# Linear attention and a maxout FFN on one core: the softmax sums of batches 4 to 7 through DMA transposes and VectorE

## The chip, the core and the metric

The kernel runs on one core of a Trainium2 chip. Each engine (TensorE or PE for matrix products, VectorE or DVE, ScalarE or ACT, GpSimd or POOL, SyncE or SP, which here only issues DMAs) follows its own instruction list in order, and waits on semaphores for the others. The metric is the device time of one execution in microseconds, lower is better. Times that are compared with each other are medians over several executions.

## What is computed

An attention whose keys and values are first projected along the sequence from 1024 to 64 rows (matrices E and F), for 8 batches of 8 heads with head width 64. Its output, with the heads side by side, is the input of 8192 rows by 512 of a feed-forward block, where the largest of three products is taken element by element.

```python
k_proj = einsum('ks,bhsd->bhkd', E, k)
v_proj = einsum('ks,bhsd->bhkd', F, v)
scores = q @ k_proj.T / sqrt(64)
attn = exp(scores - max) / sum(exp(scores - max))      # over the 64 projected keys
x = (attn @ v_proj) with heads side by side             # 8192 x 512
h = max(max(x @ w1, x @ w2), x @ w3)                    # 512 -> 768
out = h @ w_out                                         # 768 -> 512
```

The kernel takes the exponential without subtracting the maximum, and divides after the product with v_proj: it multiplies by the inverse of the sum over the 64 keys.

## The kernel before, in words

One loop runs over the 8 batches b, and in each turn over two chunks of 512 rows. A chunk has 10 steps: six `up` steps (each makes one 128-wide slice of h: three groups of four 128x128x512 matmuls, one for each of w1, w2 and w3), then four `down` steps (six matmuls each, the product with w_out for 128 rows). In a step of `up`, ACT copies the first product from PSUM (h1s, L754), VectorE takes the larger of it and the second (m, L758), then of that and the third (hT, L699). `down` reads hT, ACT copies its result to o_sb, and after every second `down` SP issues a store of two results (L813).

The attention of the next batch, n = b + 1, is woven between these steps. The function `plan(b)` holds the order: a key (chunk, step) gives the list of functions that are called behind that step. [...] Eight PSUM banks are dealt out by a small planner, which keeps a model clock for TensorE, ACT and VectorE (`runs`, `pe`) and gives the bank that it expects to be free first. The numbers in `runs(...)` and `when` steer only this choice.

For loop turns b = 3 to 6, which prepare batches 4 to 7, the order is:

- behind (0, 1): the scores of head pairs 1 to 3 of batch n (`sc`); ACT makes the exponentials, tile pT (L230): for each pair of heads, 128 partitions (64 keys for each of two halves of the rows) by 1024. Pair 0 was made at the end of the turn before.
- behind (0, 3): `zc(n)`. Eight small matmuls (L264) with the 0/1 matrix `pick` add pT over the keys, for all head pairs, into one bank. ACT takes the logarithm (L270) and the exponential of its negative (L273), which gives the inverse. SP writes the result to a scratch buffer zd in DRAM (L276, 32 KB) and reads it back four times (L283, 512 KB each), spread over 64 partitions by a broadcast: tile zi_all.
- behind (0, 4): `qd(n + 1)`, for batches up to 7: VectorE copies q of the batch after next into q_p (L102), and SP issues a DMA transpose of 1 MB from q_p to qT (L422).
- behind (1, 2): `kvproj(n + 1)` (the projections of k and v; SP then transposes k by DMA to kpT, L538), and `vx` for pairs 0 and 1: the product of pT and v_proj (L239), and on VectorE its multiplication by zi_all into xT (L316).
- behind (1, 3): `ld(n + 2)`: GpSimd issues the loads of q, k and v for a later batch (L201), which convert from fp32 to bf16 on their way. The load of q waits for the DMA transposes qT and kpT of the batch before it (`last_T`, `turned`).
- behind (1, 6): `vx` for pairs 2 and 3, then the scores of pair 0 of batch n + 1.

SP's list in such a turn is therefore: zd, four zi_all, qT, the two stores of the first chunk, kpT, the two stores of the second chunk. In b = 6 there are no qT, kpT and loads. q_t has two buffers, k_t and v_t have one each, pT has six, zi_all one.

Of the kernel before, what the change touches and what calls it, by code (L numbers as in the profile page):

```python
# [8 lines left out]
FP32 = mybir.dt.float32  # L9
BF16 = mybir.dt.bfloat16  # L10
AF = mybir.ActivationFunctionType
ALU = mybir.AluOpType
# [3 lines left out]
def kernel(  # L16
# [13 lines left out]
    nc = tc.nc  # L30
# [7 lines left out]
    P = 128  # L38
    HALF = 64
# [3 lines left out]
    NPAIR = H // 2  # L43
    CHUNK = 512
    NCHUNK = S // CHUNK
    SPC = SI // NCHUNK
# [5 lines left out]
    att = ctx.enter_context(tc.tile_pool(name="att", bufs=2))  # L52
    scratch = ctx.enter_context(
        tc.tile_pool(name="scratch", bufs=2, space=bass.MemoryType.DRAM)
    )
# [26 lines left out]
    def bank():  # L82
        n = min(range(8), key=lambda n: free[n])
        deal((n,))
        return psum_t[:, n, :], (n,)

    def pe(dt, wait=0.0):
        clock["pe"] = max(clock["pe"], wait) + dt
        return clock["pe"]

    def runs(eng, ready, dt, ns=()):
        if eng in clock:
            clock[eng] = max(clock[eng], ready + 0.06) + dt
            for n in ns:
                free[n] = clock[eng]
            return clock[eng]
        return ready + dt
# [33 lines left out]
    qkv, qTs, kpTs, vps, pTs, zis, xTs = {}, {}, {}, {}, {}, {}, {}  # L131
# [119 lines left out]
    def zi_all(b):  # L251
        if b not in zi_alls:
            zi_alls[b] = att.tile([P, NPAIR, 2, CHUNK], FP32, name="zi_all", bufs=1)
        return zi_alls[b]

    def zc(b, queue=nc.sync):

        def f():  # L260
            t, ns = bank()
            for hp in range(2):
                for g in range(NPAIR):
                    nc.tensor.matmul(  # L264
                        out=t[32 * g:32 * (g + 1), :], lhsT=pick[:, hp, :],
                        rhs=pTs[b, g, 0][:, hp, :], start=(hp == 0), stop=(hp == 1),
                    )
            ready = pe(2 * MM + 0.1)
            zlc = att.tile([P, CHUNK], FP32, name="zlc", bufs=1)
            nc.scalar.activation(out=zlc, in_=t, func=AF.Ln)  # L270
            runs("s", ready, 0.6, ns)
            zic = att.tile([P, CHUNK], FP32, name="zic", bufs=1)
            nc.scalar.activation(out=zic, in_=zlc, func=AF.Exp, scale=-1.0)  # L273
            when = runs("s", ready, 0.63) + 9.0
            zd = scratch.tile([NPAIR, 2, 2, CHUNK], FP32, name="zd")
            nc.sync.dma_start(  # L276
                out=zd.rearrange("g h c f -> (g h c) f"),
                in_=zic.rearrange("(a r) f -> a r f", r=8)[:, 0, :],
            )
            for u in range(2):  # L280
                gs = slice(2 * u, 2 * u + 2)
                for hp in range(2):
                    queue.dma_start(  # L283
                        out=zi_all(b)[hp * HALF:(hp + 1) * HALF, gs],
                        in_=zd[gs, hp].partition_broadcast(HALF),
                    )
            for g in range(NPAIR):
                zis[b, g, 0] = zi_all(b)[:, g], when
        return f
# [39 lines left out]
    def sc(b, g, lo=0, nsi=SI, now=False):  # L329
        def f():  # L330
            t = scores(b, g, lo, nsi)
            if now:
                exps(b, g, lo, nsi, t)
            else:
                later.append(lambda: exps(b, g, lo, nsi, t))
        return f
# [72 lines left out]
    def qd(b, gs=range(NPAIR), eng="v"):  # L409

        def f():
            lo, n = gs[0], len(gs)
            if lo == 0:
                q_ps[b] = att.tile([P, NPAIR, SI, 2, D], BF16, name="q_p", bufs=1)
                qTs[b] = att.tile([P, NPAIR * SI, P], BF16, name="qT")
            q_p = q_ps[b]
            for g in gs:
                copy(
                    eng, q_p[:, g].rearrange("p si h d -> p h si d"),
                    qkv[b][0][:, 2 * g:2 * g + 2], (), 0.43,  # L420
                )
            last_T[b] = nc.sync.dma_start_transpose(  # L422
                out=qTs[b][:, lo * SI:(lo + n) * SI, :],
                in_=q_p[:, lo:lo + n].rearrange("p g si h d -> p (g si h d)"),
            )
        return f
# [67 lines left out]
    def kproj(b):  # L494
        def f():
            t, ns = bank()
            proj(b, 1, t, (LO, HI), 4 * D)
            kps[b] = att.tile([P, 2, 2 * D], BF16, name="kp")
            copy("v", kps[b].rearrange("a g x -> a (g x)"), t[:, 0:4 * D], ns, 0.43)
        return f  # L500

    def kt(b):
        def f():
            t, ns = two()
            t = t.bitcast(BF16)[:, 0]
            for gg in range(2):
                nc.tensor.transpose(
                    out=t[:, gg * P:(gg + 1) * P], in_=kps[b][:, gg, :], identity=ident
                )
            pe(0.2)  # L510

            kpTs[b] = att.tile([P, NPAIR, KP], BF16, name="kpT")
            copy(
                "v", kpTs[b].rearrange("a (y x) k -> a x y k", x=2),
                t[:, 0:2 * P].rearrange("a (x y k) -> a x y k", x=2, y=2), ns, 0.3,
            )
        return f
# [32 lines left out]
    def vproj(b):  # L550
        def f():
            t, ns = bank()
            proj(b, 2, t, (LO, HI), 4 * D)

            vps[b] = att.tile([P, H, D], BF16, name="vp")
            for hh, hs in enumerate((LO, HI)):
                i = t[hh * HALF:(hh + 1) * HALF, 0:4 * D].rearrange("a (h d) -> a h d", d=D)
                for to in range(2):
                    copy("sv"[hh], vps[b][to * HALF:(to + 1) * HALF, hs, :], i, ns, 0.4)
        return f  # L560
# [266 lines left out]
    def ld(b, which=(0, 1, 2)):  # L827
        return lambda: load(b, which)

    def plan(b):  # L830
        n = b + 1
        if b == 0:
            return {
                (0, 6): [
                    duo[1].sums, duo[1].values, duo[0].scale, duo[1].invert,
                ],
                (0, 7): [
                    qd(1, range(2)), duo[1].scale, qd(1, range(2, 4), "s"), store_now,
                ],
                (1, 1): [kproj(1)],  # L840
                (1, 2): [kt(1)],
                (1, 3): [sc(1, 0, now=True), sc(1, 1), vproj(1), ld(2)],
                (1, 4): [za(1, 0), sc(1, 2, now=True)],
                (1, 5): [za(1, 1)],
                (1, 6): [sc(1, 3, now=True)],
                (1, 7): [za(1, 2)],
                (1, 8): [za(1, 3)],
            }
        if b == 1:
            return {  # L850
                (0, 0): [qd(2)],
                (0, 3): [kproj(2), vproj(2), ld(3, (0,))],
                (0, 4): [kt(2)],
                (0, 5): [sc(2, 0, now=True), sc(2, 1, now=True), sc(2, 2)],
                (0, 6): [sc(2, 3, now=True)],
                (0, 8): [zc(2, nc.gpsimd), ld(3, (1, 2))],
                (1, 1): [qd(3)],
                (1, 3): [vx(2, 0), vx(2, 1)],
                (1, 6): [vx(2, 2), vx(2, 3)],
            }  # L860
        if b == 2:
            return {
                (0, 2): [kproj(3), vproj(3), ld(4)],
                (0, 3): [kt(3)],
                (0, 4): [sc(3, 0, now=True), sc(3, 1)],
                (0, 5): [sc(3, 2, now=True), sc(3, 3, now=True)],
                (0, 7): [zc(3)],
                (0, 8): [qd(4)],
                (1, 3): [kproj(4), vproj(4), ld(5), vx(3, 0), vx(3, 1)],
                (1, 4): [kt(4)],  # L870
                (1, 8): [vx(3, 2), vx(3, 3), sc(4, 0)],
            }
        if n == B:
            return {}
        out = {
            (0, 1): [sc(n, 1, now=True), sc(n, 2, now=True), sc(n, 3)],
            (0, 3): [zc(n)],
            (1, 2): [vx(n, 0), vx(n, 1)],
            (1, 6): [vx(n, 2), vx(n, 3)],
        }  # L880
        if n + 1 < B:
            out[0, 4] = [qd(n + 1)]
            out[1, 2] = [kvproj(n + 1)] + out[1, 2]
            out[1, 6] += [sc(n + 1, 0)]
        if n + 2 < B:
            out[1, 3] = [ld(n + 2)]
        return out

    duo = [Duo(u, SPC) for u in range(2)]

    for b in range(B):
        p = plan(b)

        def behind(ch, step):
# [61 lines left out]
```

## Time and profile before

| quantity | value |
|---|---|
| median of 3 runs | 399.08 us (398.91 to 399.47) |
| the profiled execution, its own time | 399.08 us |
| its span, first to last instruction | 397.3 us |
| granted TensorE clock | 1.00 |
| eight matmuls of `zc` in b = 3 (L264) | 180.01 to 180.55 us |
| ACT: logarithm and exponential of `zc` (L270, L273), mean of one | 597 and 630 ns |
| VectorE: multiplication by zi_all (L316), mean of one | 1220 ns |
| zd written, time to landing | 1.8 to 5.5 us, median 2.5 |
| zi_all read back, time to landing | 4.9 to 10.3 us, median 7.9 |
| qT, DMA transpose of 1 MB, time to landing | 7.2 to 22.1 us, median 12.9 (two of the eight are halves) |
| DMA engines, mean busy share in the 40 slices | mostly 9 tenths until 300 us, mostly 0 to 3 from 320 us |

A loop turn takes 46.4 us here: b = 3 begins at 168.5 us, b = 4 at 214.9, b = 5 at 261.2 and b = 6 at 307.6. In lines of the timeline the columns are the start in us, the duration in us, the engine (SPq is SP issuing DMAs), the line, the operation, what is written and read, and in brackets how long the engine was idle before and what ended that. In lines of the DMA view the columns are the queue, its packets, MB, and the time of its packets as a share of 16 engines; shares over 100% occur because packets overlap on an engine.

### The profile page before, as it was taken

What the parts mean: (1) busy time and instruction counts of PE and PEld (TensorE: products, weight loads), DVE (VectorE), ACT (ScalarE), POOL (GpSimd) and SP (SyncE); (2) the same over time, 40 slices, a digit from 0 to 9 for tenths busy, and PEclk for the clock granted to TensorE, in tenths of its full rate; (3) what the DMA queues carried; (4) which work ended last, traced back from release to release, by engine and by line L of the source; (5) the groups of instructions that cost most, each with busy time, mean ns of one, the idle gap of its engine ahead of it and who ended that gap; (6) DMA issues with size and microseconds to landing.
All of it is one profiled execution on the core that took longest, in us unless ns stands there. A gap on an engine that the chain in (4) does not pass through costs nothing.

```text
span 397.3 us, 5598 instructions
## 1 busy us (share of the span) xinstructions
PE 386.9 (97%) x2196; PEld 173.5 (44%) x2238; DVE 202.4 (51%) x309; ACT 151.9 (38%) x236; POOL 34.3 (9%) x49
## 2 busy tenths in 40 slices
PE   7899999999999999999999999999999999999996
PEld 3544443453445445444444444444444444444443
DVE  3348756751764525645374544845266443745251
ACT  2434638527222552263323532245323533132322
POOL 7350001000401100200011000200000000000000
PEclk9999999999999999999999999999999999999999
DMA  8999999987999998999979969597971138020202
GB/s 146 206 206 207 205 237 151 245 160 161 231 183 263 165 211 205 220 180 210 214 202 160 245 151 270 100 240 124 217 210 43 64 89 234 2 106 0 107 0 106
DMA packets 67338, 66.29 MB, mean 167 GB/s; under 512 B 31504, under 2 KB 59792, under 8 KB 67312
## 3 DMA queue, kind: packets, MB, share of 16 engines
q0 software_dynamic: 29104, 30.41, 47.4%
q1 hardware_dynamic: 38064, 35.46, 34.7%
q8 instruction: 17, 0.28, 0.3%
q10 hardware_dynamic: 144, 0.07, 0.1%
q14 instruction: 9, 0.07, 0.1%
HBM read 69.73 MB, written 16.97 MB: 218 GB/s over the span
## 4 chain that ended last, share of the span: by engine, by line
PE 90%; DMA 3%; DVE 2%; POOL 2%; issue 1%; ACT 1%; DVEq 0%; ACTq 0%; POOLq 0%
PE banks L689 61%; PE banks L797 20%; DMA v_t<-in_v_dram 3%; PE banks L239 2%; PE banks L353 2%; PE banks L219 2%; PE banks L528 1%; PE banks L264 1%; DVE xT L316 1%; DVE m L758 1%; ACT zi_all L305 1%; ACT zl L299 1%; DVE hT L699 0%; POOL k_t L152 0%; POOL q_t L157 0%
## 5 line engine op out<-in xcount | busy, mean ns | idle before, releaser
L689 PE MATMUL banks<-xT,w_sb 128*128 128x512 bf16 x1125 | 255.2, 379 | 1.9 <-DVE xT L316 0.3
L689 PEld LDWEIGHTS <-w_sb 128*128 128x128 bf16 x1152 | 110.2, 98 | 136.7 <-issue 8.4
L758 DVE TENSOR_TENSOR m<-banks,h1s 128x512 f32<-128x512 f32 x90 | 62.1, 690 | 131.4 <-ACT h1s L754 88.8
L754 ACT COPY h1s<-banks 128x512 f32<-128x512 f32 x90 | 52.6, 585 | 119.6 <-PE banks L689 119.6
L797 PE MATMUL banks<-wout_sb,hT 128*128 128x512 bf16 x364 | 85.5, 380 | 1.0 <-issue 0.3
L699 DVE TENSOR_TENSOR hT<-banks,m 128x512 bf16<-128x512 f32 x90 | 62.3, 692 | 9.7 <-DVE m L758 0.5
L797 PEld LDWEIGHTS <-hT 128*128 128x128 bf16 x378 | 35.3, 98 | 48.4 <-issue 6.1
L102 ACT COPY o_sb<-banks 128x512 f32<-128x512 f32 (+2 forms) x57 | 32.9, 577 | 58.4 <-PE banks L797 50.6
L316 DVE TENSOR_TENSOR xT<-banks,zi_all 128x1024 bf16<-128x1024 f32 x28 | 33.2, 1220 | 12.8 <-PE banks L239 8.2
L230 ACT ACTIVATE pT<-banks 128x1024 bf16<-128x1024 f32 (+1 forms) x32 | 30.2, 975 | 16.2 <-PE banks L219 16.2
L201 POOL DMA_DIRECT2D q_t<-in_q_dram x7 | 6.1, 878 | 197.3 <-DMA qT<-q_p 84.9
L102 ACT CAST vp<-banks 64x256 bf16<-64x256 f32 (+1 forms) x11 | 4.7, 424 | 20.5 <-DVE kp L102 11.2
L102 DVE CAST vp<-banks 64x256 bf16<-64x256 f32 (+2 forms) x15 | 6.7, 445 | 10.0 <-ACT vp L102 7.3
L239 PE MATMUL banks<-pT,vp 64*64 64x512 bf16 (+1 forms) x128 | 10.3, 375 | 0.5 <-DVE vp L102 0.2
L102 DVE COPY q_p<-q_t 128x1024 bf16<-128x1024 bf16 x26 | 9.8, 437 | 0.0
L219 PE MATMUL banks<-qT,kpT 64*64 64x512 bf16 (+1 forms) x128 | 9.7, 372 | 0.0
L102 DVE CAST kp<-banks 128x256 bf16<-128x256 f32 (+2 forms) x9 | 4.6, 509 | 8.8 <-PE banks L528 3.5
L102 DVE COPY o_sb<-banks 128x512 f32<-128x512 f32 (+1 forms) x9 | 5.6, 640 | 5.4 <-PE banks L777 4.5
L299 ACT ACTIVATE zl<-banks 128x512 f32<-128x512 f32 (+1 forms) x8 | 6.5, 810 | 2.9 <-PE banks L239 2.7
L353 PEld LDWEIGHTS <-efT 128*64 128x64 bf16 x128 | 6.6, 110 | 2.1 <-issue 2.1
L567 PE MATMUL banks<-warm_f 128*128 128x512 f32 x8 | 5.9, 877 | 1.5 <-DVE warm_f L175 1.5
L201 POOL DMA_DIRECT2D v_t<-in_v_dram x7 | 6.3, 900 | 1.0 <-PE banks L689 1.0
(76 smaller groups left out, 136.3 us busy)
## 6 DMA issues: line engine op xcount, KB each, us to landing
out_dram<-o_sb SPq DMA_DIRECT2D x30, 512.0 KB, 3.9
zi_all<-zd SPq DMA_DIRECT2D x20, 512.0 KB, 7.9
q_t<-in_q_dram POOLq DMA_DIRECT2D x7, 1024.0 KB, 9.8
k_t<-in_k_dram POOLq DMA_DIRECT2D x7, 1024.0 KB, 17.1
v_t<-in_v_dram POOLq DMA_DIRECT2D x7, 1024.0 KB, 21.9
zi_all<-zd POOLq DMA_DIRECT2D x4, 512.0 KB, 7.6
w_sb<-in_moe_w_dram POOLq DMA_DIRECT2D x4, 384.0 KB, 11.0
k_t<-in_k_dram POOLq DMA_DIRECT2D x2, 512.0 KB, 9.1
```

The source lines that it names most:

```text
L102: done = {"v": nc.vector.tensor_copy, "s": nc.scalar.copy, "g": nc.gpsimd.tensor_copy}[eng](out=o, in_=i)
L201: dma = nc.gpsimd.dma_start(out=tiles[i], in_=view((q, k, v)[i], b))
L219: nc.tensor.matmul(out=t[c * HALF:(c + 1) * HALF, hp, 0:n * P], lhsT=k_pair(b, g)[rows], rhs=qTs[b][rows, at:at + n, :], start=True, stop= ...
L230: nc.scalar.activation(out=pTs[b, g, lo], in_=t, func=AF.Exp, scale=scale)
L239: nc.tensor.matmul(out=t[hp * HALF:(hp + 1) * HALF, c, 0:nsi * HALF], lhsT=w(rows, hp), rhs=p[rows, hp, :], start=True, stop=True,)
L316: nc.vector.tensor_tensor(out=xTs[b][:, g, lo:lo + nsi, :].rearrange("a (c s) p -> a c (s p)", c=2), in0=t, in1=zi, op=ALU.mult,)
L353: nc.tensor.matmul(out=t[hh * HALF:(hh + 1) * HALF, 0:width], lhsT=efT[:, si, (kv - 1) * KP:kv * KP], rhs=qkv[b][kv][:, heads[hh], si, :], ...
L689: nc.tensor.matmul(out=h, lhsT=w_sb[i][:, ct, jt * P:(jt + 1) * P], rhs=xTs[b][:, ct, ch * SPC:(ch + 1) * SPC, :], start=(ct == first), st ...
L699: nc.vector.tensor_tensor(out=o, in0=h, in1=other, op=ALU.max)
L754: nc.scalar.copy(out=h1s, in_=h[0][0])
L758: nc.vector.tensor_tensor(out=m12, in0=h[1][0], in1=h1s, op=ALU.max)
L797: nc.tensor.matmul(out=o_ps, lhsT=hTs[b, ch][:, jt, tt * P:(tt + 1) * P], rhs=wout_sb[:, jt, :], start=(jt == 0), stop=(jt == NJT - 1),)
```

## The change

For batches 4 to 7, `zc(n)` is no longer called (batches 2 and 3 keep it). Three new functions do its work:

- `turn_p`: SP issues a DMA transpose of each pT tile (128x1024 bf16, 256 KB) into p_T, eight blocks of 128x128 in which the rows of the sequence lie on the partitions and the keys along the free dimension. p_T uses the buffers of the tile zi0.
- `sum_p`: VectorE adds over the 64 keys, 1024 elements in and 16 out per partition (tile s_T).
- `spread_z`: VectorE inverts the 64 sums per partition (zr), transposes the 128x64 tile in 32x32 blocks (zt), SP writes zt to zd with two DMAs in pieces of 32 numbers, and reads it back with the same four zi_all DMAs as before.

Their places in the plan: pair 0 is turned behind (0, 0), pairs 1 to 3 behind (0, 2), the sums are made behind (0, 5), (0, 6) and (0, 7), and the spreading follows behind (0, 7). `qd(n + 1)` stays behind (0, 4). SP's list in such a turn becomes: four turns of pT, qT, the first store, two zd writes, four zi_all, the second store, kpT, the stores of the second chunk.

```diff
+    def turn_p(b, g):
+        def f():
+            if b not in s_T:
+                s_T[b] = att.tile([P, NPAIR, 2, SPC, 2], FP32, name="s_T")
+            p_T[b, g] = att.tile([P, 2, CHUNK // 2], FP32, name="zi0", bufs=4).rearrange(
+                "p a f -> p (a f)"
+            ).bitcast(BF16).rearrange("p (n x) -> p n x", x=P)
+            nc.sync.dma_start_transpose(
+                out=p_T[b, g], in_=pTs[b, g, 0].rearrange("p h f -> p (h f)")
+            )
+        return f
+
+    def sum_p(b, g):
+        def f():
+            nc.vector.tensor_reduce(
+                out=s_T[b][:, g].rearrange("p h s c -> p (h s) c"),
+                in_=p_T[b, g].rearrange("p n (c k) -> p n c k", c=2),
+                axis=mybir.AxisListType.X, op=ALU.add,
+            )
+            runs("v", 0.0, 1.15)
+        return f
+
+    def spread_z(b, queue=nc.sync):
+        def f():
+            n = NPAIR * 4 * SPC
+            zr = att.tile([P, n], FP32, name="zr")
+            nc.vector.reciprocal(
+                out=zr.rearrange("p (a c s) -> p a c s", c=2, s=SPC),
+                in_=s_T[b].rearrange("p g h s c -> p (g h) c s"),
+            )
+            zt = att.tile([P, n], FP32, name="zt")
+            nc.vector.transpose(out=zt, in_=zr)
+            when = runs("v", 0.0, 0.35) + 11.0
+            zd = scratch.tile([NPAIR, 2, 2, CHUNK], FP32, name="zd")
+            rows = zd.rearrange("g h c (s a r) -> (g h c s) a r", a=4, r=32)
+            for j in range(2):
+                nc.sync.dma_start(
+                    out=rows[32 * j:32 * (j + 1)].rearrange("i a r -> a i r"),
+                    in_=zt[:, 32 * j:32 * (j + 1)],
+                )
...
         out = {
             (0, 1): [sc(n, 1, now=True), sc(n, 2, now=True), sc(n, 3)],
-            (0, 3): [zc(n)],
+            (0, 0): [turn_p(n, 0)],
+            (0, 2): [turn_p(n, 1), turn_p(n, 2), turn_p(n, 3)],
+            (0, 5): [sum_p(n, 0), sum_p(n, 1)],
+            (0, 6): [sum_p(n, 2)],
+            (0, 7): [sum_p(n, 3), spread_z(n)],
             (1, 2): [vx(n, 0), vx(n, 1)],
             (1, 6): [vx(n, 2), vx(n, 3)],
         }
```

More of the change, by code (lines that the diff above doesn't have):

```diff
@@ L279, in f @@
             )
+            for u in range(2):
+                gs = slice(2 * u, 2 * u + 2)
+                for hp in range(2):
+                    queue.dma_start(
+                        out=zi_all(b)[hp * HALF:(hp + 1) * HALF, gs],
+                        in_=zd[gs, hp].partition_broadcast(HALF),
+                    )
+            for g in range(NPAIR):
+                zis[b, g, 0] = zi_all(b)[:, g], when
+        return f
+    s_T, p_T = {}, {}
+    def turn_p(b, g):
[17 more added lines that the diff above has]
+            runs("v", 0.0, 1.15)
+        return f
+    def spread_z(b, queue=nc.sync):
[15 more added lines that the diff above has]
+                    in_=zt[:, 32 * j:32 * (j + 1)],
+                )
             for u in range(2):
```

## The prediction, made before the changed kernel ran

> **What bounds the kernel now.** I read the busy shares first, then the chain of waits, then the timeline of loop turn b=4 (batch 5 is prepared there, span 215 to 261 us), and last the DMA view in stretches of 2 us.
>
> ```profile
> PE 386.9 (97%) x2196; PEld 173.5 (44%) x2238; DVE 202.4 (51%) x309; ACT 151.9 (38%) x236; POOL 34.3 (9%) x49
> PE 90%; DMA 3%; DVE 2%; POOL 2%; issue 1%; ACT 1%; DVEq 0%; ACTq 0%; POOLq 0%
> ```
>
> TensorE is never free for long: it is busy 97% of the span and holds 90% of the chain that ended last. So a TensorE instruction that goes is worth its whole time, and any wait that reaches TensorE costs its whole time too. The next view, VectorE's timeline late in b=4, tells how near such a wait is:
>
> ```profile
> 249.25 2.36 DVE L316 TENSOR_TENSOR xT<-banks,zi_all 128x1024 bf16<-128x1024 f32 x2
> 251.52 0.68 DVE L758 TENSOR_TENSOR m<-banks,h1s 128x512 f32<-128x512 f32 x1
> 252.31 0.69 DVE L699 TENSOR_TENSOR hT<-banks,m 128x512 bf16<-128x512 f32 x1
> 252.92 0.68 DVE L758 TENSOR_TENSOR m<-banks,h1s 128x512 f32<-128x512 f32 x1
> 253.70 0.69 DVE L699 TENSOR_TENSOR hT<-banks,m 128x512 bf16<-128x512 f32 x1
> 254.80 0.69 DVE L758 TENSOR_TENSOR m<-banks,h1s 128x512 f32<-128x512 f32 x1 [0.40 <-PE banks L689]
> 255.59 0.69 DVE L699 TENSOR_TENSOR hT<-banks,m 128x512 bf16<-128x512 f32 x1
> ```
>
> From the first multiplication by zi_all to the last hT tile VectorE is idle for only 0.40 us, and the down product that follows already waited 0.20 us for that hT. So if zi_all comes late, TensorE loses the delay less 0.4 us.
>
> Now the queue that brings zi_all. SP's timeline in the same turn, and the same transpose in three surroundings:
>
> ```profile
> 228.35 0.54 SPq L276 DMA_DIRECT2D zd<-zic  x1
> 231.50 2.55 SPq L283 DMA_DIRECT2D zi_all<-zd  x4
> 234.16 10.73 SPq L422 DMA_TRANSPOSE qT<-q_p  x1
> 244.99 1.00 SPq L813 DMA_DIRECT2D out_dram<-o_sb  x2
> ...
> 78.46 5.76 SPq L422 DMA_TRANSPOSE qT<-q_p  x1
> ...
> 105.31 19.73 SPq L422 DMA_TRANSPOSE qT<-q_p  x1
> ```
>
> A DMA transpose holds SP while it is issued: 5.76 us with free engines (it lands after 7.5), 10.73 us behind zi_all, 19.73 us beside loads (lands after 22.1). The DMA view says why; here are 118 to 120 us, inside the 19.73, and 82 to 84 us, inside the 5.76:
>
> ```profile
> q0 software_dynamic: 307, 0.31, 91.3%
> q1 hardware_dynamic: 308, 0.08, 29.7%
> ...
> q1 hardware_dynamic: 2195, 0.56, 124.9%
> ```
>
> q0 carries the loads in packets of 1 KB, q1 (SP's) the transpose in packets of 256 bytes. Alone, q1 moves 2195 packets in 2 us; beside loads 308, one for one with q0.
>
> **What the Trainium skill says.** "DMA: Bandwidth & Descriptors", section "Queues, rings and completion order": each DMA engine goes round its queue rows packet by packet, and takes one row's descriptors in ring order. The trace agrees: 307 against 308 above, and in b=4 qT, issued at 234.16, shows its small packets only from about 242 us, when zi_all is through. The same page, section "Anatomy of one DMA — SWDGE (gpsimd) path": DMA engines don't wait on semaphores, the issuing sequencer does; so everything behind a waiting DMA on SP waits too (in the trace zi_all is issued at 231.50, on zd's landing 3.1 us after its issue). "VectorE: DVE Perf Modes", section "The perf-mode tier table": tensor_reduce runs at one element a cycle whatever the type. No reduction is in this trace, but the multiplication over 128x1024 is 1.22 us at that pace.
>
> **The change, part by part** (batches 4 to 7, prepared in b=3 to 6).
>
> *Removed.* Eight matmuls of L264: 180.08 to 180.62 us in the chain, 0.54 us with the gap; four times 2.2 us, all on TensorE. Two ACT passes (0.60 + 0.63 us) and the old 32 KB zd write go; ACT was idle beside them, nothing for the time.
>
> *Added on VectorE.* Four sums at 1.22 us are 4.9 us a batch, behind the last hT of the first chunk (233.2 us in b=4). VectorE has no work from there to 240.3 us, so 7.1 us cover them if the turned tiles are in. Reciprocal and transpose of 128x64: the 128x64 memset is 0.11 us, a 128x128 fp32 copy 0.29; between 0.2 and 0.8 for both, I take 0.4.
>
> *Added on SP, in its order:* four turns of 1024 packets each, then qT (4096), the store of the first two down results, two zd writes (0.54 us each by the old one), four zi_all (2.55 us). Before, zd and zi_all were ahead of qT. The turns of 256 KB each issue in 1.4 us when free (a quarter of 5.76), and 6.8 us beside loads (1024 at 150 a us). The loads of a batch, some 3,100 packets, occupy q0 from about 210 to 230 us in b=4 and from 168 to 190 in b=3, just where the turns come. zd in 128-byte pieces: old landings are 1.8 to 5.5 us; I take 2.8 from the second issue. zi_all: in b=4 its four landings were 5.0 to 10.0 us after their issues, so the first half (two DMAs) is in about 7.3 us after the first issue, the second after 11.9.
>
> Sum for batch 4 (b=3): the stores before it leave the ring at about 177 us. From there q0 has 2,193 packets left (sum of the stretches to 190). At 150 a us each, loads and turns share until 191.6; 1,900 turn packets remain and take 2.7 us at 711 a us (4096 in 5.76 us): 194.3. SP leaves the turns at about 193, qT takes it to 198.8, store and zd to 200.2; zd lies behind qT and the store in the ring and lands at 203.0. First half of zi_all: 210.3. It is wanted at 202.86 less the 0.54 saved, 202.3. Stall 8.0, on TensorE 7.6. The sums end near 197.7, 4 us after VectorE had its next work, which the eight banks just cover.
>
> Batch 5: the next q load waits for kpT, which lies behind zi_all in the ring; it starts 9.1 us later, 2.0 more than TensorE's own delay. So q0 has 1,453 + 360 packets left at 222 us, shares until 234.1, turns end at 237.3, qT is issued 236.0 to 241.8, zd lands 246.0, zi_all 253.3 against 248.7: stall 4.6, cost 4.2.
>
> Batch 6, by the same steps (load 3.9 us later than its turn, 1,868 packets left at 268): turns end 283.6, qT 282.3 to 288.1, zd 292.3, zi_all 299.6 against 295.1: stall 4.5, cost 4.1.
>
> Batch 7 has neither loads nor a qT. The sums start at 325.3 and end with the inversion at 330.5; zd lands 333.3, zi_all 340.6 against 338.1. In b=6 VectorE has 1.8 us of waits to catch up: cost 0.7.
>
> Total: 7.6 + 4.2 + 4.1 + 0.7 - 2.2 = +14.4 us. The profiled span is 397.3 and that run took 399.08, which is also the median; so 413.5 us.
>
> **Rivals.** *The turns are hidden (faster).* If a turn gets through beside loads at its free pace (1.4 us), the four of batch 4 are in by 184, qT is issued 185.4 to 191.2, the sums end at 191.5, zi_all is there at 202.7 against 202.3; only the 2.2 us remain, some given back: 397.5 us. For it: a turn is a quarter of a qT, and its sums have a gap of their own. Against it: the 308 packets. It decides as soon as zi_all lands within 0.4 us of its need. *Only batch 4 loses.* If the turns of batches 5 and 6 are in by 232 and 278 us, qT starts when its copies are ready (231.8) and zi_all lands at 248.9, in time; batch 4 still gives 5 to 8: 402 to 405 us. *VectorE and the small zd pieces bind as well (slower still).* Every 1 us that the last turn or zd lands later is passed on in three batches. The page on DMA, section "Why a DMA increments its semaphore by 16 and not by 1", spreads a DMA over as many engines (16 at most) as divide both slowest dimensions; zd's destination has 4 outermost, so an estimate is four engines instead of sixteen. With 3 us each: 423 us. Against it: it is only 128 pieces in each.
>
> **How the numbers follow.** Forecast (zi_all late in three batches) 0.58, 405 to 421 us; the heavier case 0.18; only batch 4 0.12; hidden, faster, 0.12. The range 401 to 424 leaves out the faster case and the tail of the heavier one. 0.2% of 399 (0.8 us) is about what a measurement of this kernel can tell from no change: faster 0.12, same 0.02, slower 0.86.
>
> **What would show it.** Right: turns issued 4 to 7 us long in b=3, and the last one landing near 195 us; SP's qT ahead of zd and near 5.8 us long; VectorE's multiplication waiting on the DMA zi_all<-zd for some 8, 4.6 and 4.5 us; the wait of the down product's weights on hT grown by as much; b=6 nearly whole. Wrong: turns of 1.5 us beside loads, or no wait of xT on zi_all. If VectorE waits mainly on the turned tiles instead, or kpT's late landing holds the next scores, the place is wrong though the sign is right.

## The result

| kernel | median, us | lowest to highest | against the kernel before |
|---|---|---|---|
| before | 399.25 | 398.91 to 399.47 | |
| changed | 412.4 | 411.15 to 412.97 | 1.033 [1.030, 1.035] |

The change makes the kernel 13.2 us slower. The profiled execution is the fastest of the four: 411.15 us, span 409.2, where the kernel before has 399.08 and 397.3. First the page's busy shares and shares of the chain of waits:

```profile
PE 390.8 (96%) x2206; PEld 174.1 (43%) x2206; DVE 223.0 (54%) x333; ACT 147.6 (36%) x228; POOL 34.3 (8%) x49
PE 75%; DMA 14%; DVE 5%; issue 2%; POOL 1%; ACT 1%; SPq 0%; DVEq 0%; ACTq 0%; POOLq 0%
```

TensorE's share of the chain falls from 90% to 75%, and DMA's rises from 3% to 14%. Note that TensorE's busy time rose by 3.9 us although it has 32 matmuls less to do (the count of PE doesn't show that, since the trace misses some records; the weight loads, 2238 before and 2206 here, do). Part of that rise is only apparent, because 42 matmul records are missing before and none here; the rest comes back below. The places are found by cutting the span at the first `up` matmul of each loop turn:

| loop turn (prepares) | before, us | changed, us | difference |
|---|---|---|---|
| b = 3 (batch 4) | 46.38 | 54.36 | +7.98 |
| b = 4 (batch 5) | 46.39 | 47.79 | +1.40 |
| b = 5 (batch 6) | 46.39 | 49.21 | +2.82 |
| b = 6 (batch 7) | 44.29 | 43.71 | -0.58 |

Together +11.6 of the span's +11.9 us. The loss is in the three turns that carry loads; the one without them gains. In b = 3, SP's timeline (the turns have the tile name zi because p_T uses its buffers):

```profile
170.99 22.41 SPq L303 DMA_TRANSPOSE zi<-pT  x4
193.50 4.88 SPq L481 DMA_TRANSPOSE qT<-q_p  x1
198.48 0.53 SPq L872 DMA_DIRECT2D out_dram<-o_sb  x1
199.10 1.36 SPq L335 DMA_DIRECT2D zd<-zt  x2
201.88 3.45 SPq L342 DMA_DIRECT2D zi_all<-zd  x4
205.42 0.54 SPq L872 DMA_DIRECT2D out_dram<-o_sb  x1
206.06 1.21 SPq L597 DMA_TRANSPOSE kpT<-kp  x1
```

The four turns hold SP for 22.4 us, qT for 4.9 more, and only then can the sums' inverse go out. In the kernel before, the four zi_all of this turn are issued at 186.59 us. This is what VectorE and TensorE make of it, in their timelines:

```profile
192.92 1.22 DVE L310 TENSOR_REDUCE s_T<-zi 128x16 f32<-128x1024 bf16 x1 [5.08 <-DMA zi<-pT]
195.17 2.35 DVE L310 TENSOR_REDUCE s_T<-zi 128x16 f32<-128x1024 bf16 x2 [1.03 <-DMA zi<-pT]
197.55 0.55 DVE L325 RECIPROCAL zr<-s_T 128x64 f32<-128x64 f32 x1
198.14 0.24 DVE L330 STREAM_TRANSPOSE zt<-zr 128x64 f32<-128x64 f32 x1
...
210.41 2.36 DVE L375 TENSOR_TENSOR xT<-banks,zi_all 128x1024 bf16<-128x1024 f32 x2 [5.94 <-DMA zi_all<-zd]
...
216.96 0.69 DVE L817 TENSOR_TENSOR m<-banks,h1s 128x512 f32<-128x512 f32 x1 [1.41 <-PE banks L748]
```

In the same place of the kernel before, TensorE's 35 recorded matmuls follow each other without a wait:

```profile
201.22 7.94 PE L689 MATMUL banks<-xT,w_sb 128*128 128x512 bf16 x35
```

In the changed kernel:

```profile
204.74 1.67 PE L748 MATMUL banks<-xT,w_sb 128*128 128x512 bf16 x7
211.69 6.03 PE L748 MATMUL banks<-xT,w_sb 128*128 128x512 bf16 x16 [5.28 <-DVE xT L375]
```

VectorE's multiplication by zi_all waits until 210.41 us, and every m and hT behind it in VectorE's list comes after it; the banks stay full, and TensorE stands for 5.28 us. Then its next 16 matmuls take 6.03 us. In b = 4 and b = 5 the same 16 take 3.61. VectorE's inverse is ready at 198.38 us, only 0.7 us before zd goes out: the turned tiles themselves landed late, and qT and the store on SP added the rest. The view of windows, with PE, PEld, DVE, ACT and POOL busy time, then the granted TensorE clock, DMA share and GB/s, shows why:

```profile
206.40:211.69 5.29, 0.01 (x2) 0.00 (x1) 1.28 (x2) 0.00 (x0) 0.00 (x0) 0.82 1.03 226
211.69:215.00 3.31, 3.31 (x8) 1.13 (x8) 3.10 (x5) 0.00 (x0) 0.00 (x0) 0.50 0.78 233
```

After the wait the clock is 0.50: the longest wait costs 6.03 - 3.61 = 2.4 us on top of itself. That is another part of the higher busy time. So b = 3 loses 5.28 + 2.42 - 0.54 (the removed matmuls) = 7.2 of the measured 8.0 us directly; two waits of 0.2 us on other VectorE results come in the same turn. In b = 4 and 5, where TensorE's waits for xT are 1.09 and 2.53 us, a `down` product later in the turn waits 0.62 us more for its hT.

Last the view of the DMA engines, 184 to 186 us (turns beside loads) and 330 to 332 us (turns in b = 6, no loads), with the turns of these two loop turns as issues (shortest, median and longest time that one holds SP, in ns):

```profile
q0 software_dynamic: 310, 0.32, 93.0%
q1 hardware_dynamic: 313, 0.07, 29.4%
...
q1 hardware_dynamic: 1576, 0.40, 101.3%
...
L303 SPq DMA_TRANSPOSE zi<-pT x4: 1531/5349/6479, 171.0 to 189.2; - x4
...
L303 SPq DMA_TRANSPOSE zi<-pT x4: 1232/1278/1522, 321.8 to 330.1; - x4
```

### The profile page after: what moved, and what is told of

Its sections match the earlier page's. It is cut to its first block, busy times and chain, and to the rows that moved or that the text cites. A ratio compares the mean times of both kernels' runs of the same rounds, so it can differ in the third digit from the quotient of the medians.

```text
span 409.2 us, 5634 instructions
## 1 busy us (share of the span) xinstructions
PE 390.8 (96%) x2206; PEld 174.1 (43%) x2206; DVE 223.0 (54%) x333; ACT 147.6 (36%) x228; POOL 34.3 (8%) x49
## 4 chain that ended last, share of the span: by engine, by line
PE 75%; DMA 14%; DVE 5%; issue 2%; POOL 1%; ACT 1%; SPq 0%; DVEq 0%; ACTq 0%; POOLq 0%
PE banks L748 50%; PE banks L856 18%; DMA zi_all<-zd 5%; DMA v_t<-in_v_dram 3%; DMA zi<-pT 3%; DMA zd<-zt 2%; PE banks L412 2%; PE banks L219 2%; DVE m L817 2%; DVE xT L375 2%; PE banks L239 2%; DVE hT L758 1%; DVE s_T L310 1%; ACT zi_all L364 1%; ACT zl L358 1%
## 5 line engine op out<-in xcount | busy, mean ns | idle before, releaser
L748 PE MATMUL banks<-xT,w_sb 128*128 128x512 bf16 x1152 | 259.4, 382 | 9.5 <-DVE xT L375 9.2
L856 PE MATMUL banks<-wout_sb,hT 128*128 128x512 bf16 x378 | 87.3, 380 | 1.4 <-DVE hT L758 1.2
L375 DVE TENSOR_TENSOR xT<-banks,zi_all 128x1024 bf16<-128x1024 f32 x28 | 33.2, 1220 | 27.3 <-DMA zi_all<-zd 14.9
L310 DVE TENSOR_REDUCE s_T<-zi 128x16 f32<-128x1024 bf16 x16 | 18.7, 1212 | 11.0 <-DMA zi<-pT 11.0
```

Of the source, the lines that this page charges most:

```text
L310: nc.vector.tensor_reduce(out=s_T[b][:, g].rearrange("p h s c -> p (h s) c"), in_=p_T[b, g].rearrange("p n (c k) -> p n c k", c=2), axis=m ...
L375: nc.vector.tensor_tensor(out=xTs[b][:, g, lo:lo + nsi, :].rearrange("a (c s) p -> a c (s p)", c=2), in0=t, in1=zi, op=ALU.mult,)
L748: nc.tensor.matmul(out=h, lhsT=w_sb[i][:, ct, jt * P:(jt + 1) * P], rhs=xTs[b][:, ct, ch * SPC:(ch + 1) * SPC, :], start=(ct == first), st ...
L856: nc.tensor.matmul(out=o_ps, lhsT=hTs[b, ch][:, jt, tt * P:(tt + 1) * P], rhs=wout_sb[:, jt, :], start=(jt == 0), stop=(jt == NJT - 1),)
```

## The experiments

Three theories were stated before the runs. A: zi_all is late because the turns crawl beside the loads and everything behind them on SP waits, and TensorE pays that lateness. B: the added VectorE work costs. C: the turns' own traffic costs, wherever they are.

### The parts alone

**e2_sums_alone**: `zc` stays, VectorE makes sums, inverse and transpose from pT directly, and nothing uses them. No turns.

```diff
-                in_=p_T[b, g].rearrange("p n (c k) -> p n c k", c=2),
+                in_=pTs[b, g, 0].rearrange("p h f -> p (h f)").rearrange(
+                    "p (n c k) -> p n c k", c=2, k=HALF
+                ),
...
-            (0, 0): [turn_p(n, 0)],
-            (0, 2): [turn_p(n, 1), turn_p(n, 2), turn_p(n, 3)],
+            (0, 3): [zc(n)],
```

> The kernel before, zc and zi_all untouched, plus the added VectorE work alone for batches 4 to 7: four reductions, the reciprocal and the 32x32 transpose, at their places in the changed kernel, reading pT as it is (so the sums are not those over keys) and used by nothing. Theory A: 5.6 us of work in a gap of 7.1 us, no change, 399 to 400 us. Theory B: 4 to 12 us more than before.

Measured 399.59 us, ratio 1.0008 [1.0002, 1.0015]: 0.3 to 0.4 us for all four batches. B falls.

**e3_turns_alone**: `zc` stays, and the 16 turns are made where nothing waits for them.

```diff
+            (0, 3): [zc(n)],
+        out[1, 3] = out[1, 3] + [turn_p(n, g) for g in range(NPAIR)]
```

> The kernel before, zc and zi_all untouched, plus the sixteen DMA transposes of pT alone, used by nothing and issued behind kpT, at (1, 3), so that zd, zi_all, qT and kpT keep their places. Theory A: the transfers cost nothing by themselves, 399 to 401 us. Theory C (the added 4 MB of traffic slows the loads and all else): 405 us or more.

Measured 399.0 us, ratio 0.9997 [0.9989, 1.0006]. At this place the traffic costs nothing, so C falls as it was stated ("wherever they are"). The run does not test the turns in their own place, since most of them are issued here before the next loads get going. SP's timeline in b = 3:

```profile
204.09 5.53 SPq L303 DMA_TRANSPOSE zi<-pT  x4
```

That is 5.5 us for four turns instead of 22.4. Whether the turns, beside the loads, delay the loads so that somebody waits can be read from the changed kernel: from 165 us on its view of waits has none of TensorE, VectorE or ACT on a load.

### Without the loads

**e5_before_no_loads** and **e5_after_no_loads**: the same edit in both kernels. It leaves out the loads of batches 5 to 7, which are then computed from the tiles of batch 4, so the output is not the wanted one; the time alone is of use.

```diff
     def load(b, which):
+        if b >= 5:
+            if b not in qkv:
+                qkv[b] = qkv[b - 1]
+            return
```

> The kernel before with the loads of q, k and v for batches 5 to 7 left out (those batches compute with the tiles of batch 4). It is the base line of the next run. Nothing waits for these loads in the kernel before: 399 us, at most 1 us less.

> The changed kernel with the same loads left out (batches 5 to 7 compute with the tiles of batch 4), so no load runs beside the turns of batches 4 to 7. Theory A: a turn is issued in 1.3 to 1.5 us instead of 3 to 6.5, the turns are in before qT's copies are ready, qT is issued at once, the sums run without a wait in their gap, and zi_all lands within 1 us of its need in all batches: 397 to 399 us, 1 to 2 us faster than the base line without loads. If the order on SP alone were the cause (qT ahead of zd), VectorE would still wait 3 us or more for zi_all in batches 4 to 6: 405 us or more. Theory B: 412 us.

Measured 399.47 us for the first (1.0012 [1.0005, 1.0018] of the kernel before) and 397.15 us for the second (0.9953 [0.9938, 0.9968]). So without the loads the change *gains* 2.3 us, and the prediction's removed matmuls were 2.2. SP's timeline of b = 3 and the turns as issues, then VectorE's sums and its multiplication by zi_all:

```profile
170.35 10.15 SPq L307 DMA_TRANSPOSE zi<-pT  x4
184.74 4.68 SPq L485 DMA_TRANSPOSE qT<-q_p  x1
...
191.47 1.28 SPq L339 DMA_DIRECT2D zd<-zt  x2
193.54 2.60 SPq L346 DMA_DIRECT2D zi_all<-zd  x4
...
L307 SPq DMA_TRANSPOSE zi<-pT x4: 1232/1285/2399, 170.3 to 179.2; - x4
```

```profile
185.98 4.59 DVE L314 TENSOR_REDUCE s_T<-zi 128x16 f32<-128x1024 bf16 x4
202.12 2.36 DVE L379 TENSOR_TENSOR xT<-banks,zi_all 128x1024 bf16<-128x1024 f32 x2
```

Neither line of VectorE has a wait. The slow turns need the loads beside them; that is shown. (Without the loads zi_all and qT have the DMA engines to themselves too, so the 15 us by which this run is faster than the changed kernel are not due to the turns alone.) It is no way to use the change, since the loads have to be made.

### Can the order be mended?

**e1_qT_behind**: qT is issued on SP behind zi_all instead of in front.

```diff
-            out[0, 4] = [qd(n + 1)]
+            out[0, 4] = [qd_pack(n + 1)]
+            out[0, 7] += [qd_turn(n + 1)]
```

`qd_pack` is the part of `qd` that makes the copies to q_p, `qd_turn` the DMA transpose.

> The changed kernel with one order altered: the DMA transpose qT is issued behind the four zi_all instead of ahead of zd; its copies to q_p stay where they were. Theory A (zi_all is late because of what stands before it on SP, and TensorE pays the lateness): zd is issued when the VectorE work on the sums ends, 0.7 us earlier for batch 4, 1.4 for batch 5, 0.9 for batch 6, and lands some 0.8 us sooner because qT's data is no longer ahead of it in the ring; together 5 us less, of which up to 2 may be given back where qT and kpT now land close to the next scores: 407.5 to 410 us. Theory B (the VectorE work itself is what costs): unchanged, 412 us. If qT were the main cost, the wait of xT on zi_all would vanish in all three batches: 401 us.

Measured 421.37 us, ratio 1.0555 [1.0533, 1.0577]: a clear miss, 9 us slower than the change. SP's and VectorE's timelines, then the view of waits:

```profile
197.53 1.27 SPq L335 DMA_DIRECT2D zd<-zt  x2
199.60 2.60 SPq L342 DMA_DIRECT2D zi_all<-zd  x4
202.29 11.25 SPq L500 DMA_TRANSPOSE qT<-q_p  x1
213.63 0.53 SPq L890 DMA_DIRECT2D out_dram<-o_sb  x1
214.22 1.43 SPq L615 DMA_TRANSPOSE kpT<-kp  x1
...
207.07 2.36 DVE L375 TENSOR_TENSOR xT<-banks,zi_all 128x1024 bf16<-128x1024 f32 x2 [3.47 <-DMA zi_all<-zd]
...
PEld L219 <- DMA kpT<-kp: 11.7, 3, 4.6
```

zi_all came earlier, as meant (5.94 us of wait became 3.47). Here zd goes out as soon as VectorE has the inverse (197.50 us), so by an estimate from these two waits qT in front was worth some 2.5 us, and the 3.47 left come from the turned tiles and the transfers behind the sums. But behind 2 MB of zi_all qT holds SP for 11.25 us, kpT goes out at 214.22 instead of 206.06, and the scores of the next batch wait for kpT in three turns. The expectation had looked at one transfer of the queue and not at the one after.

**e6_vx_late**: zi_all is wanted later; `vx` of pairs 0 and 1 goes three steps back.

```diff
-            (1, 2): [vx(n, 0), vx(n, 1)],
+            (1, 5): [vx(n, 0), vx(n, 1)],
```

> The changed kernel with the first two multiplications by zi_all moved from (1, 2) to (1, 5), some 8 us later; nothing else. Theory A: the waits of xT on zi_all (5.9, 2.7, 4.2, 2.1 us) vanish, but kpT, which stays behind zi_all in SP's ring, now comes too late for the next scores at (1, 6), as in the run with qT behind: TensorE waits there for kpT 4 us in batch 4 and 1 to 3 us in batches 5 and 6. 404 to 408 us. If only the wait on zi_all mattered: 398 us. Theory B: 412 us.

Measured 414.01 us, ratio 1.0376 [1.0346, 1.0405]: a miss again. The second path was expected this time, but too cheap. The view of waits, then TensorE's timeline in b = 3 and in b = 5:

```profile
DVE xT L375 <- DMA zi_all<-zd: 4.4, 3, 2.2
...
PEld L219 <- DMA kpT<-kp: 11.4, 3, 4.9
...
215.86 0.64 PE L219 MATMUL banks<-qT,kpT 64*64 64x512 bf16 x4 [4.36 <-DMA kpT<-kp]
217.26 5.90 PE L856 MATMUL banks<-wout_sb,hT 128*128 128x512 bf16 x16 [0.22 <-issue]
...
316.91 0.41 PE L219 MATMUL banks<-qT,kpT 64*64 64x512 bf16 x4 [4.62 <-DMA kpT<-kp]
...
317.93 5.07 PE L856 MATMUL banks<-wout_sb,hT 128*128 128x512 bf16 x16 [0.22 <-issue]
```

The wait on zi_all fell from 14.9 to 4.4 us in all, and 11.4 us of wait on kpT stand in its place. After the waits in b = 3 and b = 5, 16 `down` matmuls take 5.90 and 5.07 us, where 18 take 4.06 in the changed kernel; the expectation had nothing for that. kpT lies behind all four zi_all in SP's ring. In the changed kernel this was covered by the wait for zi_all.

**e7_vx_late_kpT_early**: e6, and kpT goes between the two halves of zi_all: `spread_z` issues the first half, and the second (kept in `halves`) is issued behind `kvproj`.

```diff
-            out[1, 2] = [kvproj(n + 1)] + out[1, 2]
+            out[1, 2] = [kvproj(n + 1), lambda: halves.pop()()] + out[1, 2]
```

> As the run with the late multiplications, and the second half of zi_all (head pairs 2 and 3) is issued behind kpT instead of ahead of it. Theory A: kpT lands some 5 us earlier, about when the next scores want it, and both lateness paths are covered: 397.5 to 400 us, as fast as the kernel before or up to 2 us faster. If the lateness sits elsewhere (the sums on VectorE, the turns' traffic), it stays above 405 us.

Measured 404.46 us, ratio 1.0137 [1.0119, 1.0154], 4 to 7 us above the expected. Almost 10 us of e6 are recovered, and the waits of the scores on kpT are down from 11.4 to 0.8 us, which shows the second path. It isn't all: in b = 3 the second half of zi_all is now late.

```profile
216.28 2.36 DVE L381 TENSOR_TENSOR xT<-banks,zi_all 128x1024 bf16<-128x1024 f32 x2 [4.68 <-DMA zi_all<-zd]
```

**e9_second_half_later**: e7, with `vx` of pairs 2 and 3 behind (1, 8).

```diff
-            (1, 6): [vx(n, 2), vx(n, 3)],
+            (1, 8): [vx(n, 2), vx(n, 3)],
```

> All four batches on the new path in that order, and the multiplications by the second half of zi_all moved from (1, 6) to (1, 8). Theory A: batch 4's wait of 4.7 us of VectorE for it shrinks to at most 1 us: 398.5 to 401 us. If batch 4 cannot be covered (its kpT, sums or loads come too late as well): 403 us or more.

Measured 401.62 us, ratio 1.0064 [1.0046, 1.0083], just above the expected range; b = 3 is 47.55 us long against 51.35 in e7. TensorE still waits there 1.02 us for kpT and 0.92 for xT. Of the 13.2 us 10.8 are recovered by order alone, but no order tried made the kernel faster than before while a batch with loads beside its turns took the new path.

### Batch by batch

**e8_batches5to7_reordered**: batch 4 keeps `zc`, batches 5 to 7 run in e7's order.

```diff
+        if n == 4:
+            out = {
+                (0, 1): [sc(n, 1, now=True), sc(n, 2, now=True), sc(n, 3)],
+                (0, 3): [zc(n)],
+                (1, 2): [vx(n, 0), vx(n, 1)],
+                (1, 6): [vx(n, 2), vx(n, 3)],
+            }
```

> Batch 4 keeps zc and its old order; batches 5 to 7 take the new path in the order of the previous run (first multiplications at (1, 5), kpT ahead of the second half of zi_all). Theory A: the only large wait left in that run, batch 4's for the second half of zi_all, is gone, since batch 4 is the one whose turns meet the loads longest; three batches save their eight matmuls and give most of it back in small waits around (1, 6): 397.5 to 399 us, the same as or slightly faster than the kernel before.

Measured 400.64 us, ratio 1.0035 [1.0022, 1.0049]: slower than expected. Two waits of VectorE on the second half of zi_all, 2.70 us in b = 4 and 2.65 in b = 5, reach TensorE (1.17 and 1.12 us) and come with losses around them: b = 4 and b = 5 are 1.2 and 1.1 us longer than before although each saves its eight matmuls.

**e10_batches5to7**: batch 4 keeps `zc`, the rest is the change as it was (the edit for n == 4 is that of e8). It asks whether b = 4 and 5 lose only because b = 3 had lost.

> The change as it was, but for batches 5 to 7 only; batch 4 keeps zc and its order. It tells what batch 4 costs by itself and whether its lateness is handed on through the loads. If it isn't handed on, the result is the changed kernel less the 8.0 us by which batch 4's loop turn grew: 404 us. Theory A has it handed on (the next loads start later, so the next turns meet more of them): the waits of batches 5 and 6 shrink as well, to 0 to 3 us each, 399 to 403 us.

Measured 405.7 us, ratio 1.0161 [1.0141, 1.018]. Neither side was right. By loop turn:

| | b = 3 | b = 4 | b = 5 | b = 6 |
|---|---|---|---|---|
| changed, against before | +7.98 | +1.40 | +2.82 | -0.58 |
| e10, against before | 0 | +0.77 | +6.47 | -0.49 |

The losses don't add. The timelines point to what is handed on: the start of the next q load against TensorE. GpSimd's timeline of e10, late in b = 4, and SP's and TensorE's in b = 5:

```profile
258.12 0.88 POOL L201 DMA_DIRECT2D q_t<-in_q_dram  x1 [48.12 <-DMA kpT<-kp]
...
263.27 22.01 SPq L303 DMA_TRANSPOSE zi<-pT  x4
...
302.77 6.28 PE L748 MATMUL banks<-xT,w_sb 128*128 128x512 bf16 x16 [4.30 <-DVE xT L375]
```

The load waits for the late kpT. Before, it was issued 9.5 us ahead of b = 5; in the changed kernel 5.1 us, in e10 4.0. So in e10 more of it meets the turns, they take 22.0 us instead of 20.4, the wait is 4.30 us instead of 2.53, and the clock falls again (16 matmuls 6.28 us). So a turn in which TensorE itself loses time brings the loads back into step and shelters the next one. This is read from the timelines; no run moved the load alone.

**e4_batch7_only**: only batch 7, the one without loads beside its turns, gets the change.

```diff
+            (0, 3): [zc(n)],
...
+        if n == B - 1:
+            out.update({
+                (0, 0): [turn_p(n, 0)],
+                (0, 2): [turn_p(n, 1), turn_p(n, 2), turn_p(n, 3)],
+                (0, 3): [],
+                (0, 5): [sum_p(n, 0), sum_p(n, 1)],
+                (0, 6): [sum_p(n, 2)],
+                (0, 7): [sum_p(n, 3), spread_z(n)],
+            })
```

> The change for batch 7 alone; batches 4 to 6 keep zc. In that loop turn there are neither loads nor a qT. Theory A: the eight matmuls go (0.54 us) and the lateness of zi_all (2.1 us) is caught up by VectorE: 0.5 to 0.8 us faster than before, 398.6 us. Theory B: slower by 1 us or more.

Measured 398.58 us, ratio 0.9985 [0.9978, 0.9993]. As expected, but by loop turn the profile keeps little of it: b = 6 takes 44.23 us against 44.29. Chunk 0 is 0.65 us shorter, chunk 1 0.59 longer; a `down` product there waits for hT:

```profile
346.74 0.39 PE L856 MATMUL banks<-wout_sb,hT 128*128 128x512 bf16 x1 [0.42 <-DVE hT L758]
```

**e11_batch7_later**: e4, with `vx` of pairs 0 and 1 one step later.

```diff
+            (1, 2): [],
+            (1, 3): [vx(n, 0), vx(n, 1)],
```

> The change for batch 7 alone, with its first two multiplications by zi_all moved from (1, 2) to (1, 3). In the run with batch 7 alone the first chunk of that loop turn became 0.65 us shorter and the second 0.59 us longer, as VectorE waited 2.6 us before the multiplication. Theory A: with 2.7 us more for zi_all that wait and the give-back go: 0.5 us faster than that run, 398.0 to 398.5 us. If the second chunk stays long, the give-back isn't the wait on zi_all.

Measured 398.24 us (397.77 to 398.41, seven runs), before 399.28, ratio 0.9974 [0.9963, 0.9986]. The wait of `down` is gone, and b = 6 takes 43.64 us. This version is about 1 us faster than the kernel before; 0.65 us of that is seen in b = 6. It is the best that was found with the loads in place; without them the idea was worth 2.3 us for four batches (e5).

## Why the prediction was right, step by step

The forecast was 413.5 us, range 401 to 424, slower with a chance of 0.86; the median is 412.4. The mechanism and the places held in the main; some sizes didn't, and one cost was missing.

- *Turns and loads share packet by packet.* Right: 310 and 313 packets in 2 us, where 307 and 308 were read from the old qT. The rule in the Trainium skill, "DMA: Bandwidth & Descriptors", section "Queues, rings and completion order", that a DMA engine goes round its queues packet by packet, could be carried from one transfer to another. 6.8 us a turn was a little high (median 5.35 in b = 3, longest 6.48); 1.4 us alone was right (1.23 to 1.52 in b = 6).
- *Batch 4: SP out of the turns at about 193, qT 5.8 us, first half of zi_all 210.3.* Measured 193.4, 4.9 and 210.3 us; the last was partly luck. zd landed at 201.8 instead of 203.0, and the first half of zi_all then took 8.4 us instead of 7.3. The sums ended at 197.5 us (forecast 197.7), and as forecast the banks covered that: TensorE waited 0.19 us for them. The stall was called 8.0 us on VectorE; its own wait reads 5.94, because it had already arrived late after waiting 6.1 us for turned tiles. Against the need that was forecast, 202.3 us, zi_all is 8.1 us late, of which 0.6 is that the loop turn itself began later (169.25 us, before 168.68). Cost: 8.5 us (7.98 + the 0.54 saved) against 7.6.
- *"TensorE loses the delay less 0.4 us".* Not right in mechanism. VectorE's 5.94 us in b = 3 became 5.28 on TensorE, and the halved clock added 2.4, which the prediction put at nothing: a wait cost more than its whole time. In b = 4 and b = 5 VectorE made up 1.0 us instead of 0.4 (2.70 us became 1.09 + 0.62, and 4.16 became 2.53 + 0.62).
- *Batch 5, stall 4.6, cost 4.2.* The mis-sized term. The loads were to start 2.0 us later against the turn; they started 0.2 later (7.3 us ahead of it, 7.5 before), since the load came only 8.7 us later and not 9.1, and b = 4 began 8.6 us later and not 7.1. The stall was 2.70 us and the cost 1.40 + 0.54 = 1.9.
- *Batch 6, load 3.9 us later, stall 4.5, cost 4.1.* Load 4.4 us later (5.1 against 9.5), stall 4.16, cost 3.4.
- *Batch 7, cost 0.7.* VectorE did wait 2.08 us for zi_all, but there it caught up: the turn is 0.58 us shorter, which is nearly the whole saving.
- *Removed, 2.2 us.* Right: 2.3 without the loads. By loop turn the first chunk is 0.65 us shorter each time and not 0.54; without the loads some of it is given back.
- *VectorE's work hidden.* Right (e2). Sums 1.21 us; inversion and transpose together 0.80 us, the top of the bounds and twice the 0.4 that I took.
- *zd lands 2.8 us after its second issue.* Too long: in b = 3 zi_all, which waits for it, could be issued 2.1 us after that (2.72 us after the first issue in the chain). The rival with slow small pieces is excluded by that, "only batch 4 loses" by b = 5, and "hidden" by the turns. The hidden case is real where its condition is met, as e5 and b = 6 show.

The sum came out right partly because two errors offset each other: batches 5 to 7 were taken 3.7 us too dear (9.0 against 5.3), batch 4 0.9 too cheap, and the median lies 1.3 us above the profiled execution. That kpT lies behind zi_all as well was named only as a sign that the place is wrong; it turned out to be a second path, ready as soon as the first one is mended.

## What to carry to other kernels

Price a DMA transpose by what runs beside it: the same 256 KB held its queue for 1.3 us alone and 5.3 us beside loads, and everything behind it on that queue moved with it. When an item is moved on a shared queue, follow every transfer behind it to the instruction that needs it; here zi_all, qT and kpT each became the late one as soon as another was helped. Ask of each batch whether it has the cover that the idea needs, and apply the idea only there.

## What was not expected of the hardware

- A long wait of TensorE costs more than its own length. After waits of 5.28, 4.36 and 4.30 us the granted clock was 0.50 to 0.51; after 1.09 and 2.53 us, 16 matmuls took the usual 3.61 us. The Trainium skill, "TensorE: Matmul & The Clock Gate", section "Part 1: The HAM clock gate", gives an idle window of about 3.4 us, after which the clock is halved, and the long waits agree. But in e1 the clock was 0.57 after only 2.81 us (TensorE's timeline, then the row of these matmuls in the view of windows):

```profile
208.35 5.14 PE L766 MATMUL banks<-xT,w_sb 128*128 128x512 bf16 x16 [2.81 <-DVE xT L375]
...
208.35:212.00 3.65, 3.65 (x10) 1.33 (x10) 3.44 (x5) 0.20 (x1) 0.00 (x0) 0.57 1.12 169
```

Later in the same run TensorE waited 2.69 us for kpT, until 218.04 us, and the clock was 0.50 between 219 and 221 us. So here a wait of under 3 us was already not safe. What sets the exact point was not tried.
- The same qT of 1 MB held SP for 4.7 us without loads (e5), for 4.9 us in b = 3 of the changed kernel, and for 11.25 us behind 2 MB of zi_all (e1).
